# Two attention-and-mixer layers on one core: the planner's slack for VectorE units from 1000 to 0, and the last token tiles' normalization from VectorE to ScalarE

## The chip, the cores and the metric

The kernel runs on one core of a Trainium2 chip. The metric is the device time of one execution in microseconds. A run before the change took 1726.44 us (median of three executions, 1724.27 to 1726.56).

## What is computed

The reference applies the same pair of blocks twice, with the same weights, to one sequence of 2048 tokens with 640 features (`@` is a matrix product, all inputs are bf16):

```python
def A(x, wqkv, wo):                    # 32 heads of 20 features
    q, k, v = split(x @ wqkv)
    p = softmax(q @ k.T * 20 ** -0.5)  # per head, 2048 x 2048
    return concat_heads(p @ v) @ wo
def B(x, w1, b1, w2, b2):              # a token mixer: the products run over the 2048 tokens
    u = gelu(einsum("sd,sf->df", layernorm(x), w1) + b1)   # 1536 wide, tanh form
    return (u @ w2 + b2).T
x = x + A(layernorm(x)); x = x + B(layernorm(x))
x = x + A(layernorm(x)); x = x + B(layernorm(x))
```

## The kernel before

**The order of the work is planned in Python.** While the program is built, a planner keeps one clock per engine (`clk`), lists of jobs with a priority, a ready time and an assumed duration (`push`), and picks again and again the engine and the job that can start first; among jobs that can start at nearly the same time the lower priority number goes first (`queue_choose`, `pe_choose`). The instructions are emitted in that order, and on the chip each engine runs its own list in order, waiting on semaphores. So a constant of the planner costs nothing by itself, but it can change the order of everything that follows.

**Attention.** The scores of a layer are cut into 512 units. A unit is one query block of 512, one group of 4 heads and one tile of 128 keys, and it has 4 chunks of 128x512, one for each head of the group. Sixteen units with the same query block and group are a segment (the last segment of a layer is split into two halves by queries; the first segments of a layer are also cut, by keys). All P·V products of a segment (L927) add up in one PSUM bank, so P·V of the next segment starts only after VectorE has transposed that bank out (`f_tr`, L977). A unit's exponentials are made by one of two engines:

- *ScalarE* takes units in order; an instruction (`do_exp`, L887) does three or two chunks and writes them to one of 4 buffers `P`. Each chunk then needs one P·V matmul.
- *VectorE* takes whole units, chosen by `d_take`. It scales the 4 chunks out of PSUM (`do_J`, L840) into one of 3 buffers, and then makes 5 terms whose bit patterns, read as bf16, sum to the exponential (`do_T`, L860), each in one of 4 buffers `TT`. Each chunk needs five P·V matmuls. A term's buffer is free again after its four P·V matmuls.

**`d_take`** runs whenever fewer than two units are open and a score buffer is free. It adds up when VectorE would be done with another unit (`eta`), and gives it the first untaken unit of the earliest segment in which ScalarE would still be busy then:

```python
eta = (max(clk["DVE"], clk["PE"]) + (4 * 600.0 + NTERM * 610.0) * (d["open"] + 1) + len(t_jobs) * 610.0
       + sum(e[3] for e in jobs["DVE"]) + D_SLACK)
while si < NSEG and si <= acc["si"] + 1:
    if eta <= act_end(si): ...        # take untaken(si)[0]
    si += 1
```

`act_end(si)` is ScalarE's clock plus 453 ns for each chunk left up to the end of segment `si`, and `acc["si"]` is the segment whose P·V is under way. A unit that would be late for one segment is thus taken from the next.

**The end of a layer's attention.** When a segment is done, `normalize` transposes (`f_tr`), divides (`f_rec`, `f_mul`) and transposes back (`f_tr2`, L1012); `outproj` (L1066) multiplies by `wo` and adds the residual (L1105). Each token tile of 128 then gets its layer norm in `mix_ln`: statistics on VectorE (`stats_job`, L343 to L346), the scale `rt` and, where asked for, the shift `nmr` on GpSimd (`scale_job`, L354 to L360), and the normalized tile `h2`. Tiles 0 to 11 are long done by then; tiles 12 to 15 are the last four, 14 and 15 come after the last P·V. These two are normalized on VectorE straight from mean and scale (L1182), all others on GpSimd (L1190). Four matmuls for each pair of a hidden tile and a column half (`add_mm1_last`) then use the four tiles, VectorE adds the saved partial sums (L1325), ScalarE applies gelu (L1337), and the second product (`add_mm2`) runs on TensorE to the end of the layer. `gelu_table` (L1167 to L1170) makes ScalarE load its gelu table as soon as the last exponential is issued.

Of the kernel before, what the change touches and what calls it, by code (L numbers as in the profile page):

```python
# [14 lines left out]
ACT = mybir.ActivationFunctionType  # L15
ALU = mybir.AluOpType
# [51 lines left out]
LAT_ACT = 200.0  # L68
LAT_V = 120.0
EXP_CH = 453.0  # L70
D_SLACK = 1000.0
WIN_S = ((160.0, 160.0), (160.0, 160.0), (330.0, 160.0))
FILL_OVER = 0.0
M_F = 0.0
# [52 lines left out]
def kernel(  # L127
# [135 lines left out]
    def push(eng, prio, ready, dur, fn, ok=None, table=None):  # L263
        seq[0] += 1
        jobs[eng].append((prio, ready, seq[0], dur, fn, ok, table))
# [81 lines left out]
            then(mv, start + 950 + LAT_V)  # L347
        push("DVE", prio, ready, 950, f)

    def scale_job(prio, ready, mv, then, double, shift=True):  # L350

        def f(start):
            rt = stat.tile([128, 1], F32, name="rt")
            nc.gpsimd.tensor_scalar(out=rt[:], in0=mv[:, 1:2], scalar1=(1.0 + LN_EPS) if double else 1.0,  # L354
                                    scalar2=LN_EPS * LN_EPS if double else LN_EPS, op0=ALU.mult, op1=ALU.add)
            nc.gpsimd.tensor_tensor(out=rt[:], in0=rt[:], in1=mhalf[:], op=ALU.pow)
            nmr = None
            if double and shift:
                nmr = stat.tile([128, 1], F32, name="nmr")
                nc.gpsimd.tensor_scalar(out=nmr[:], in0=mv[:, 0:1], scalar1=rt[:, 0:1], scalar2=-1.0, op0=ALU.mult, op1=ALU.mult)  # L360
            then(rt, nmr, start + cost + 150)
        cost = 1100 if double and shift else 900
        push("POOL", prio, ready, cost, f)


    def add_fill(mms, cost, evac, ecost, ready=0.0, pr=5, ok=None, urgent=None, acost=None, eprio=2, bf16=None, on_start=None,
# [270 lines left out]
    def make_attention(L):  # L637
# [270 lines left out]
        def do_PV(start, sel):  # L908
            si = acc["si"]
            hist.append((start, 1.0))  # L910
            if acc["tile"] is None:
                acc["tile"] = ps(6, [128, 512])
            last = {}
            for it in sel:
                j = it[2]
                acc["cnt"][j] += 1
                last[j] = unassigned[si] == 0 and acc["cnt"][j] * 4 == pv_total[si]
            for part in range(2):
                for it in sel:
                    _, u, j, ap, ready, rel = it  # L920
                    qb, g, kt, half = units[u]
                    if half is None and part:
                        continue
                    dst, n = acc["tile"][32 * j:32 * j + 32, :], ((kt + part) * H + 4 * g + j) * VW
                    if half is not None:
                        dst, ap = dst[:, 0:256], ap[:, 256 * part:256 * (part + 1)]
                    pe(nc.tensor.matmul(dst, lhsT=Vaug[:, n:n + 32], rhs=ap, start=acc["cnt"][j] == 1 and not part,  # L927
                                        stop=last[j] and (half is None or part == 1), tile_position=(0, 32 * j)))
            for it in sel:
                pv.remove(it)  # L930
                pv_done[si] += 1
            end = start + PE_MM
            for it in sel:
                it[5](end)
            clk["PE"] = end
            pe_mode[0] = "col"
            if unassigned[si] == 0 and pv_done[si] == pv_total[si]:
                finish_seg(si, acc["tile"], end + LAT_PE)
                acc.update(si=si + 1, tile=None, cnt=[0] * 4, ready=1e18)
                if si + 1 == NSEG:  # L940
                    L.done = True
                    L.gelu_table()
                    if not L.nxt and L.w2_open:
                        for i in range(4, 8):
                            rW2.give(i, end + LAT_PE)
# [23 lines left out]
        def normalize(qb, g, half, src, ready, from_acc):  # L969
            final = half == 1  # L970
            q0, q1 = (0, 512) if half is None else (256 * half, 256 * half + 256)
            w = q1 - q0

            def f_tr(start):
                s1 = rT1.take()
                T1 = sb("T1", [128, w], F32, s1)
                nc.vector.transpose(out=T1[:], in_=src[:, 0:w])  # L977
                if from_acc:
                    acc["ready"] = start + 720 + LAT_V
                else:  # L980
                    sv_open[0] -= 1
                    if sv_open[0] == 0:
                        for i in range(NT_BUFS - NTSV, NT_BUFS):
                            rTT.give(i, start + 600)
                T1v = T1[:].rearrange("p (c i) -> p c i", i=32)

                def f_rec(start):
                    rden = stat.tile([128, 16], F32, name="rden")[:, 0:w // 32]
                    nc.vector.reciprocal(out=rden, in_=T1v[:, :, DH])  # L989

                    def f_mul(start):
                        s2 = rT2.take()
                        T2 = sb("T2", [128, w // 32, 32], BF16, s2)
                        eng = nc.vector if final else nc.gpsimd
                        end_ = start + (600 if final else 1450)
                        o_, a_, b_ = T2[:], T1v, rden.unsqueeze(2).to_broadcast([128, w // 32, 32])
                        if half is None:

                            o_ = o_.rearrange("p c i -> p (c i)").rearrange("p (c i b) -> p c b i", b=2, i=32)
                            a_ = T1[:].rearrange("p (c b i) -> p c b i", b=2, i=32)  # L1000
                            b_ = rden.rearrange("p (c b) -> p c b", b=2).unsqueeze(3).to_broadcast([128, w // 64, 2, 32])
                        eng.tensor_tensor(out=o_, in0=a_, in1=b_, op=ALU.mult)  # L1002
                        rT1.give(s1, end_)

                        def f_tr2(start):
                            if (qb, g) not in attnT:
                                aslot[(qb, g)] = rA.take()
                                attnT[(qb, g)] = sb("attnT", [128, 512], BF16, aslot[(qb, g)])
                            o_, i_ = attnT[(qb, g)][:, q0:q1], T2[:].rearrange("p c i -> p (c i)")
                            if half is None:  # L1010
                                o_, i_ = o_.bitcast(F32), i_.bitcast(F32)
                            nc.vector.transpose(out=o_, in_=i_)  # L1012
                            rT2.give(s2, start + 340)
                            on_normal(qb, g, half, start + 340 + LAT_V)
                        push("DVE", 0 if half is not None else 3, end_, 340, f_tr2, ok=lambda: len(rA) > 0 and L.v_left[1] == 0)
                    if final:
                        push("DVE", 0, start + 150, 600, f_mul, ok=lambda: len(rT2) > 0)
                    else:
                        push("POOL", 0, start + 150 + LAT_V, 1300, f_mul, ok=lambda: len(rT2) > 0)
                push("DVE", 1, start + 720, 170, f_rec)  # L1020
            push("DVE", 0, ready, 720, f_tr, ok=lambda: len(rT1) > 0)
# [109 lines left out]
    def make_mixer(L):  # L1131
# [28 lines left out]
        def got_last(tt, t):  # L1160
            h2l_ready[tt - NS_] = t
            L.mix_left -= 1
            if L.mix_left == NL - 1:
                add_mm1_last()
                add_mm2()

        def gelu_table():  # L1167
            nc.scalar.activation(out=warm[:, 0:1], in_=mhalf[:, 0:1], func=ACT.Gelu_apprx_tanh, scale=1.0)
            act_table[0] = "gelu"
            clk["ACT"] += 1500  # L1170

        def mix_ln(tt, x1s, ready, release):
            last = tt >= NS_

            def got_stats(mv, r):
                scale_job(1, r, mv, lambda rt, nmr, r2: apply_(mv, rt, nmr, r2), True, shift=not (last and L.done))

            def apply_(mv, rt, nmr, r):
                if nmr is None:
                    def f(start):  # L1180
                        h2[tt] = sb("h2", [128, D], BF16, tt)
                        nc.vector.tensor_scalar(out=h2[tt][:], in0=x1s[:], scalar1=mv[:, 0:1], scalar2=rt[:, 0:1],  # L1182
                                                op0=ALU.subtract, op1=ALU.mult)
                        got_last(tt, start + 550 + LAT_V)
                    push("DVE", 0, r, 550, f)
                    return

                def f(start):
# [5 lines left out]
                        release(e)  # L1194
                    (got_last if last else got_h2)(tt, e + 150)
                push("POOL", 1, r, 900, f, ok=(lambda: L.hT_dead) if tt >= NA1 else None)

            stats_job(3 if not last else 1 if L.done else 6, ready, x1s, got_stats)

        def add_mm1(k, tts):  # L1200

# [214 lines left out]
            if L.nxt:  # L1416
                L.nxt.load_wv()

        L.gelu_table = gelu_table
        L.on_hT_dead, L.mix_ln, L.on_attnT_dead, L.keys_dead = on_hT_dead, mix_ln, on_attnT_dead, keys_dead  # L1420


# [256 lines left out]
```

## Time and profile before

| | us |
|---|---|
| runs: median (lowest, highest) | 1726.44 (1724.27, 1726.56) |
| the profiled execution: its own time | 1724.27 |
| its span, first to last instruction | 1722.5 |
| TensorE busy, of the span | 1646.1 |
| ScalarE busy | 1581.0 |
| VectorE busy | 1464.6 |
| GpSimd busy | 167.5 |
| granted TensorE clock, mean | 0.995 |

PE is TensorE, PEld its weight loads, DVE VectorE, ACT ScalarE, POOL GpSimd. A row of the groups reads: line, engine, operation, output<-input tiles and their sizes, count | busy us, mean ns of one | idle time of the engine just before them, and what ended it. Instructions of an engine overlap a little, so busy time over count is a better spacing than the mean. A row of a timeline reads: start, duration, engine, line, operation, tiles, count, and in brackets the idle time before it.

In the span, attention of the first layer runs from about 24 to 798 us and of the second from about 850 to 1648 us; the mixer's last part follows each (798 to 850 us, and 1648 us to the end).

### The profile page before, as it was taken

The numbers are of one execution on the slowest core, as the hardware profiler recorded it, in microseconds if no ns is written. First come the engines' busy times: TensorE is split into PE (matmuls) and PEld (weight loads), VectorE is DVE, ScalarE is ACT, GpSimd is POOL, SyncE is SP. The second block draws the span as 40 slices with busy tenths as digits, with TensorE's granted clock in tenths as the row PEclk, the third lists the DMA queues.
The fourth block names the chain that finished last, engine by engine and source line by source line (L and its number), as shares of the span: only waits on it lengthen the run. The fifth ranks groups of instructions, "written<-read, shape, count | busy, mean of one in ns | idle before, by whom it ended". The sixth has DMA issues, their size and how long they took to land. (4 is left out here: it accounts for less than half of the span.)

```text
span 1722.5 us, 50500 instructions
## 1 busy us (share of the span) xinstructions
PE 1646.1 (96%) x21916; PEld 641.2 (37%) x21917; DVE 1464.6 (85%) x2630; ACT 1581.0 (92%) x1427; POOL 167.5 (10%) x261
## 2 busy tenths in 40 slices
PE   8999999999999999998999999999999999998989
PEld 3433333332333333335545432333333333332356
DVE  6688999999989999999444489999999888999963
ACT  7899999999999999997598899999999999999950
POOL 3100002000200020001100000110011000200010
PEclk9999999999999999999999999999999999999999
DMA  3200001000112106511422000100002120257143
GB/s 119 29 2 2 2 13 36 2 1 2 52 57 71 39 32 190 182 34 43 148 84 75 25 2 2 33 32 1 1 17 58 57 70 32 76 179 216 42 125 95
DMA packets 103295, 98.06 MB, mean 57 GB/s; under 512 B 45600, under 2 KB 79520, under 8 KB 103072
## 3 DMA queue, kind: packets, MB, share of 16 engines
q1 hardware_dynamic: 99456, 94.82, 17.8%
q8 instruction: 171, 2.80, 0.7%
q0 software_dynamic: 3616, 0.01, 0.3%
q14 instruction: 52, 0.43, 0.1%
HBM read 63.35 MB, written 31.46 MB: 55 GB/s over the span
## 5 line engine op out<-in xcount | busy, mean ns | idle before, releaser
L887 ACT ACTIVATE P<-pst 128x1536 bf16<-128x1536 f32 (+1 forms) x1335 | 1520.2, 1311 | 26.9 <-PE pst L700 14.5
L860 DVE TENSOR_SCALAR JT<-JT 128x2048 uint16<-128x2048 uint16 x950 | 636.4, 701 | 5.0 <-PE pst L927 1.8
L700 PE MATMUL pst<-QT,KT 32*128 32x512 bf16 (+1 forms) x4224 | 575.2, 377 | 40.7 <-ACT P L887 28.5
L840 DVE TENSOR_SCALAR JT<-pst 128x512 uint16<-128x512 f32 x760 | 507.4, 679 | 63.9 <-PE pst L700 61.5
L927 PE MATMUL pst<-P,Vaug 128*32 128x512 bf16 (+1 forms) x3440 | 500.6, 380 | 3.4 <-DVE T_85 L977 1.8
L927 PE MATMUL pst<-JT,Vaug 128*32 128x512 bf16 (+1 forms) x3920 | 465.7, 380 | 3.4 <-DVE T_85 L977 2.4
L700 PEld LDWEIGHTS <-KT 32*128 32x128 bf16 x4224 | 168.5, 91 | 512.2 <-issue 498.5
L927 PEld LDWEIGHTS <-Vaug 128*32 128x32 bf16 x7360 | 170.2, 94 | 297.3 <-issue 268.0
L1002 POOL TENSOR_TENSOR T_86<-T_85,rden 128x512 bf16<-128x512 f32 x64 | 67.5, 1054 | 1130.6 <-DVE rden L989 1090.8
L1066 PE MATMUL pst<-wo,attnT 128*32 128x320 bf16 x2048 | 111.3, 301 | 4.7 <-DVE attnT L1012 3.2
L456 PEld LDWEIGHTS <-W 128*32 128x32 bf16 x3384 | 89.7, 96 | 60.0 <-issue 28.8
L1488 PE MATMUL pst<-ident,zw 128*32 128x512 bf16 (+1 forms) x330 | 108.8, 380 | 0.0
L456 PE MATMUL pst<-hh,wq 128*32 128x512 bf16 x1232 | 104.3, 382 | 1.3 <-DVE JT L840 0.7
L456 PE MATMUL pst<-hh,wk 128*32 128x512 bf16 x1240 | 97.3, 381 | 1.1 <-DVE JT L840 0.6
L456 PE MATMUL pst<-x1last,W 128*32 128x320 bf16 x1536 | 80.6, 301 | 0.9 <-DVE JT L840 0.5
L1066 PEld LDWEIGHTS <-attnT 128*32 128x32 bf16 x2048 | 52.4, 96 | 42.2 <-issue 20.3
L456 PE MATMUL pst<-attnT,hh 128*32 128x320 bf16 x1196 | 60.2, 300 | 2.1 <-DVE hh L463 0.7
L463 DVE CAST KT<-pst 128x512 bf16<-128x512 f32 x53 | 36.0, 680 | 19.5 <-PE pst L456 18.3
L456 PE MATMUL pst<-JT,W 128*32 128x320 bf16 x1080 | 52.3, 300 | 0.0
L977 DVE STREAM_TRANSPOSE T_85<-pst 128x512 f32<-128x512 f32 (+1 forms) x58 | 40.0, 690 | 8.1 <-PE pst L927 8.0
L354 POOL TENSOR_SCALAR rt<-mv 128x1 f32<-128x1 f32 x64 | 13.4, 209 | 340.2 <-DVE mv L346 339.6
L463 DVE CAST Vaug<-pst 128x320 bf16<-128x320 f32 x43 | 20.6, 482 | 30.4 <-PE pst L456 21.6
(91 smaller groups left out, 878.0 us busy)
## 6 DMA issues: line engine op xcount, KB each, us to landing
W<-in_B_w_dram SPq DMA_DIRECT2D x10, 768.0 KB
W<-in_B_w_dram SPq DMA_DIRECT2D x24, 256.0 KB
xs<-in_A_x_dram SPq DMA_DIRECT2D x32, 160.0 KB
x2d<-xs SPq DMA_DIRECT2D x16, 320.0 KB
xs<-x2d SPq DMA_DIRECT2D x16, 320.0 KB
x1d_69<-xs SPq DMA_DIRECT2D x12, 320.0 KB
uacca_72<-W SPq DMA_DIRECT2D x12, 320.0 KB
W<-uacca_72 SPq DMA_DIRECT2D x12, 320.0 KB
```

The lines of the kernel that those rows point to most:

```text
L354: nc.gpsimd.tensor_scalar(out=rt[:], in0=mv[:, 1:2], scalar1=(1.0 + LN_EPS) if double else 1.0, scalar2=LN_EPS * LN_EPS if double else LN_ ...
L456: nc.tensor.matmul(out_[32 * c:32 * c + 32], lhsT=lhsT[:, 32 * c:32 * c + 32], rhs=rhs, start=start, stop=stop, tile_position=(0, 32 * c))
L463: nc.vector.tensor_copy(out=out_, in_=in_)
L700: pe(nc.tensor.matmul(dst, lhsT=k_, rhs=q_, start=True, stop=True, tile_position=(32 * j, 0)))
L840: nc.vector.tensor_scalar(out=c["jt"][:, j * 512:(j + 1) * 512], in0=Dt[:], scalar1=SCALE * LOG2E * 256.0, scalar2=127.0 * 256.0, op0=ALU. ...
L860: nc.vector.tensor_scalar(out=tt_[:], in0=c["jt"][:], scalar1=0.5, scalar2=TERM_C[i], op0=ALU.mult, op1=ALU.add)
L887: nc.scalar.activation(out=P[:, 0:n, :].rearrange("p a b -> p (a b)"), in_=St[:, 0:n, :].rearrange("p a b -> p (a b)"), func=ACT.Exp, scal ...
L927: pe(nc.tensor.matmul(dst, lhsT=Vaug[:, n:n + 32], rhs=ap, start=acc["cnt"][j] == 1 and not part, stop=last[j] and (half is None or part = ...
L977: nc.vector.transpose(out=T1[:], in_=src[:, 0:w])
L1002: eng.tensor_tensor(out=o_, in0=a_, in1=b_, op=ALU.mult)
L1066: nc.tensor.matmul(t[32 * c:32 * c + 32, 0:w], lhsT=q_, rhs=wo_pad[:, gg, c0:c1], start=(gi == 0), stop=(gi == len(gs) - 1), tile_position ...
L1488: pe(nc.tensor.matmul(dst[0:32, 0:128 * n], lhsT=zw[:, 0:32], rhs=ident[:].unsqueeze(1).to_broadcast([128, n, 128]), start=not inside, sto ...
```

## The change

1. `D_SLACK`, a term of `eta` in `d_take`, goes from 1000 to 0.
2. `h2` of the tiles that are normalized after the last P·V is made by ScalarE (an Identity activation with a scale and a bias for each partition) in place of VectorE; for that the shift `nmr` is needed for them too.
3. `nmr` is made by two GpSimd instructions (a product, then a multiplication by -1) in place of one.
4. The gelu table is asked for after the last of these four tiles has been normalized, in place of after the last P·V.
5. Priorities in VectorE's list: `f_tr2` of the two half segments goes from 0 to 3, and the statistics of last tiles that come before the last P·V from 6 to 1.

```diff
-D_SLACK = 1000.0
+D_SLACK = 0.0
...
 def scale_job
-                nc.gpsimd.tensor_scalar(out=nmr[:], in0=mv[:, 0:1], scalar1=rt[:, 0:1], scalar2=-1.0, op0=ALU.mult, op1=ALU.mult)
+                nc.gpsimd.tensor_tensor(out=nmr[:], in0=mv[:, 0:1], in1=rt[:], op=ALU.mult)
+                nc.gpsimd.tensor_scalar(out=nmr[:], in0=nmr[:], scalar1=-1.0, scalar2=None, op0=ALU.mult)
...
 def do_PV
                 if si + 1 == NSEG:
                     L.done = True
-                    L.gelu_table()
...
 def normalize
-                        push("DVE", 0 if half is not None else 3, end_, 340, f_tr2, ok=...)
+                        push("DVE", 3, end_, 340, f_tr2, ok=...)
...
 def got_last
                 add_mm1_last()
                 add_mm2()
+            if L.mix_left == 0:
+                nc.scalar.activation(out=warm[:, 0:1], in_=mhalf[:, 0:1], func=ACT.Gelu_apprx_tanh, scale=1.0)
+                act_table[0] = "gelu"
+                clk["ACT"] += 1500
...
 def mix_ln, apply_
-                if nmr is None:
+                if last and L.done:
-                        nc.vector.tensor_scalar(out=h2[tt][:], in0=x1s[:], scalar1=mv[:, 0:1], scalar2=rt[:, 0:1],
-                                                op0=ALU.subtract, op1=ALU.mult)
-                        got_last(tt, start + 550 + LAT_V)
-                    push("DVE", 0, r, 550, f)
+                        nc.scalar.activation(out=h2[tt][:], in_=x1s[:], func=ACT.Identity, bias=nmr[:, 0:1], scale=rt[:, 0:1])
+                        got_last(tt, start + 730 + LAT_ACT)
+                    push("ACT", 0, r, 730, f)
...
-            stats_job(3 if not last else 1 if L.done else 6, ready, x1s, got_stats)
+            stats_job(3 if not last else 1, ready, x1s, got_stats)
```

More of the change, by code (lines that the diff above doesn't have):

```diff
@@ L348, in stats_job, with scale_job @@
         push("DVE", prio, ready, 950, f)
-    def scale_job(prio, ready, mv, then, double, shift=True):
+    def scale_job(prio, ready, mv, then, double):
         def f(start):
@@ L357, in f @@
             nmr = None
-            if double and shift:
+            if double:
                 nmr = stat.tile([128, 1], F32, name="nmr")
-                nc.gpsimd.tensor_scalar(out=nmr[:], in0=mv[:, 0:1], scalar1=rt[:, 0:1], scalar2=-1.0, op0=ALU.mult, op1=ALU.mult)
-            then(rt, nmr, start + cost + 150)
-        cost = 1100 if double and shift else 900
-        push("POOL", prio, ready, cost, f)
+                nc.gpsimd.tensor_tensor(out=nmr[:], in0=mv[:, 0:1], in1=rt[:], op=ALU.mult)
+                nc.gpsimd.tensor_scalar(out=nmr[:], in0=nmr[:], scalar1=-1.0, scalar2=None, op0=ALU.mult)
+            then(rt, nmr, start + (1250 if double else 900) + 150)
+        push("POOL", prio, ready, 1250 if double else 900, f)
     def add_fill(mms, cost, evac, ecost, ready=0.0, pr=5, ok=None, urgent=None, acost=None, eprio=2, bf16=None, on_start=None,
@@ L1014, in f_tr2 @@
                             on_normal(qb, g, half, start + 340 + LAT_V)
-                        push("DVE", 0 if half is not None else 3, end_, 340, f_tr2, ok=lambda: len(rA) > 0 and L.v_left[1] == 0)
+                        push("DVE", 3, end_, 340, f_tr2, ok=lambda: len(rA) > 0 and L.v_left[1] == 0)
                     if final:
@@ L1165, in got_last @@
                 add_mm2()
[L1167 to L1170, printed above, removed]
+            if L.mix_left == 0:
+                nc.scalar.activation(out=warm[:, 0:1], in_=mhalf[:, 0:1], func=ACT.Gelu_apprx_tanh, scale=1.0)
+                act_table[0] = "gelu"
+                clk["ACT"] += 1500
         def mix_ln(tt, x1s, ready, release):
@@ L1175, in got_stats, with apply_ @@
             def got_stats(mv, r):
-                scale_job(1, r, mv, lambda rt, nmr, r2: apply_(mv, rt, nmr, r2), True, shift=not (last and L.done))
-            def apply_(mv, rt, nmr, r):
-                if nmr is None:
+                scale_job(1, r, mv, lambda rt, nmr, r2: apply_(rt, nmr, r2), True)
+            def apply_(rt, nmr, r):
+                if last and L.done:
                     def f(start):
                         h2[tt] = sb("h2", [128, D], BF16, tt)
-                        nc.vector.tensor_scalar(out=h2[tt][:], in0=x1s[:], scalar1=mv[:, 0:1], scalar2=rt[:, 0:1],
-                                                op0=ALU.subtract, op1=ALU.mult)
-                        got_last(tt, start + 550 + LAT_V)
-                    push("DVE", 0, r, 550, f)
+                        nc.scalar.activation(out=h2[tt][:], in_=x1s[:], func=ACT.Identity, bias=nmr[:, 0:1], scale=rt[:, 0:1])
+                        got_last(tt, start + 730 + LAT_ACT)
+                    push("ACT", 0, r, 730, f)
                     return
@@ L1417, in on_attnT_dead @@
                 L.nxt.load_wv()
-        L.gelu_table = gelu_table
         L.on_hT_dead, L.mix_ln, L.on_attnT_dead, L.keys_dead = on_hT_dead, mix_ln, on_attnT_dead, keys_dead
```

## The prediction

> **What bounds the kernel now.** I read the page's busy times first, then its groups, then a table of two long stretches of attention, then ScalarE's waits in one of them.
>
> ```profile
> PE 1646.1 (96%) x21916; PEld 641.2 (37%) x21917; DVE 1464.6 (85%) x2630; ACT 1581.0 (92%) x1427; POOL 167.5 (10%) x261
> ...
> L887 ACT ACTIVATE P<-pst 128x1536 bf16<-128x1536 f32 (+1 forms) x1335 | 1520.2, 1311 | 26.9 <-PE pst L700 14.5
> L860 DVE TENSOR_SCALAR JT<-JT 128x2048 uint16<-128x2048 uint16 x950 | 636.4, 701 | 5.0 <-PE pst L927 1.8
> ...
> L840 DVE TENSOR_SCALAR JT<-pst 128x512 uint16<-128x512 f32 x760 | 507.4, 679 | 63.9 <-PE pst L700 61.5
> ...
> L1488 PE MATMUL pst<-ident,zw 128*32 128x512 bf16 (+1 forms) x330 | 108.8, 380 | 0.0
> ```
>
> TensorE's 96% is no bound: 108.8 us of it are matmuls on zeros (L1488), issued where it had nothing to do. ScalarE's exponentials are 1520.2 us. There are 1024 units; 760 scaled chunks at 4 a unit make 190 units on VectorE, so ScalarE has 834 units, 3336 chunks, 1520.2 / 3336 = 0.456 us each and 1.82 us a unit. On VectorE a unit takes 4 x 507.4/760 + 5 x 636.4/950 = 2.67 + 3.35 = 6.02 us.
>
> ```profile
> 150.00:798.00 648.00, 623.62 (x8249) 216.53 (x8244) 615.18 (x1070) 639.12 (x564) 60.37 (x80) 0.99 0.16 49
> 1000.00:1648.00 648.00, 621.78 (x8232) 218.93 (x8230) 606.81 (x1057) 639.88 (x563) 59.20 (x82) 1.00 0.19 57
> ```
>
> The columns are the stretch, its length, then busy time (and instructions) of PE, PEld, DVE, ACT and POOL. In 1296 us ScalarE is idle for 8.9 + 8.1 = 17.0 us, VectorE for 32.8 + 41.2 = 74.0 us. ScalarE is the bound here, with VectorE close behind. The time can change in three ways: units move between the two, ScalarE waits more, or the stretches outside attention change.
>
> ```profile
> ACT P L887 <- PE pst L927: 4.2, 8, 1.2
> ACT P L887 <- PE pst L700: 4.0, 8, 1.2
> ```
>
> These are ScalarE's waits from 150 to 798 us: total, times, longest. It waits for P·V to free a P buffer (L927) or for scores queued behind P·V on TensorE (L700). The second layer has 6.8 us in 17 waits, so a wait is 15.0 / 33 = 0.45 us.
>
> **The slack.** Its unit is planned at 4 x 600 + 5 x 610 = 5.45 us and takes 6.02, so the chip falls 0.57 us behind the plan with each unit, 1.1 us with two open. The slack of 1.0 us covers that. Here is the end of a segment where it did not:
>
> ```profile
> 1264.83 8.23 ACT L887 ACTIVATE P<-pst 128x1536 bf16<-128x1536 f32 x7
> ...
> 1269.26 1.89 DVE L860 TENSOR_SCALAR JT<-JT 128x2048 uint16<-128x2048 uint16 x3
> ...
> 1271.22 0.61 PE L927 MATMUL pst<-JT,Vaug 128*32 128x512 bf16 x8
> ...
> 1272.26 0.71 DVE L977 STREAM_TRANSPOSE T_85<-pst 128x512 f32<-128x512 f32 x1
> ...
> 1273.02 0.40 PE L927 MATMUL pst<-P,Vaug 128*32 128x512 bf16 x4 [0.65 <-DVE T_85 L977]
> ...
> 1273.77 2.37 ACT L887 ACTIVATE P<-pst 128x1024 bf16<-128x1024 f32 x2 [0.72 <-PE pst L700]
> ```
>
> The segment's last exponential ends at 1269.5, its last VectorE term at 1271.15, the transpose starts at 1272.26, and the next segment's first P·V at 1273.02. ScalarE ran ahead on its 4 buffers and then stood still for 0.72 us. I went through the timeline in this way for the 54 whole segments between 143 and 776 us and between 992 and 1627 us (a segment's chunks are counted off its P·V matmuls). In 8 the last term ends 0.1 to 1.7 us after the last exponential. At 18 starts of a segment the opposite is seen: a unit put into the next segment has its fifth term held until 3.5 to 4.2 us after the last exponential of the segment before, since only 4 term buffers exist and none is freed before the next P·V opens.
>
> How many decisions change: a unit changes its segment where its planned end lies in the last 1.0 us before `act_end`. A segment takes about 23.4 us and holds 3.3 units, so units end 7.1 us apart: 1.0/7.1 x 54 = 8. All 18 held units are the upper bound; I take 10, between them and nearer to 8. Each now ends its segment at the planned end of ScalarE or just before it, which on the chip is later by the lag of 0.57 to 1.1 us. The segment's transpose, all P·V of the next segment behind it on TensorE, and the P buffers that these free come later by as much. ScalarE's 4 buffers hide some of it: the price is between 0 and 1.0 us each, and ScalarE's wait of 0.45 us is the nearest row; I take 0.4. That is 10 x 0.4 = +4.0 us, with 0 and 18 us as ends. The gain on the other side, units no longer held, is the third case below. The slack does not decide whether a unit is taken in the middle of a layer: a unit refused for one segment goes to the next, where 20 us and more are left. Only at a layer's end can a unit be won, at most one each.
>
> **The last tiles' normalization.** The end of the second layer, by engine:
>
> ```profile
> 1653.14 0.19 POOL L354 TENSOR_SCALAR rt<-mv 128x1 f32<-128x1 f32 x1 [3.75 <-DVE mv L346]
> 1653.42 0.55 POOL L356 TENSOR_TENSOR rt<-rt,mhalf 128x1 f32<-128x1 f32 x1
> ...
> 1654.36 0.56 DVE L1182 TENSOR_SCALAR hh<-x1last,mv,rt 128x640 bf16<-128x640 f32 x1
> 1655.63 0.61 DVE L1182 TENSOR_SCALAR hh<-x1last,mv,rt 128x640 bf16<-128x640 f32 x1 [0.72 <-POOL rt L356]
> ...
> 1654.97 11.68 PE L453 MATMUL pst<-hh,KT 128*128 128x320 bf16 x84 [1.75 <-DVE hh L1182]
> ...
> 1649.52 0.20 ACT L1168 ACTIVATE warm<-mhalf 128x1 f32<-128x1 f32 x1
> 1657.61 4.76 ACT L1337 ACTIVATE JT<-hh,b_t 128x640 bf16<-128x640 f32 x6 [7.89 <-issue]
> ```
>
> TensorE waits for tile 14 until 1654.97; then it has nine matmuls of 0.139 us that need only tile 14, which carries it to tile 15 at 1656.24. From there it never stops, so what delays tile 15 delays the end. New chain: GpSimd's power for tile 14 ends at 1653.97. The product (one-element GpSimd product in the set-up: 0.19 us) and the multiplication by -1 (0.19 as L354 to 0.26 as L360) with two gaps of 0.09 end at 1654.61. Tile 15's statistics are there at 1654.44; scale, power, product and multiplication take 0.19 + 0.55 + 0.20 + 0.26 with gaps of 0.09 and end at 1656.2. ScalarE takes the 0.83 us of the gelu rows, the same shape with a bias for each partition, and ends at 1657.03: 0.8 us later than 1656.24. The first layer's end has the same spacing (its two VectorE normalizations stand at 804.03 and 805.30), so 2 x 0.8 = +1.6 us. Below: 2 x 0.4 if the product hides in gaps. Above: a gelu chain that becomes late, next.
>
> **The gelu table** is loaded from 1648.22 for 1.28 us, and the first gelu is at 1657.61, so 8 us cover it. Now it starts behind tile 15: 1657.03 + 1.28 + 0.20 = 1658.5, when the first gelu, moved by 0.8, would be due at 1658.4. It costs 0.1 us, which the chain's later waits for VectorE (0.26 us before each of the last gelus) take up: nothing. The Trainium skill ("ScalarE: Activation LUTs", What ACT_TABLE_LOAD costs) puts a switch at 1.28 us of load and 1.38 us of drain; the row shows the load and the next activation 0.02 us behind it. By the page the tails would cost up to 1.4 us more each, 2.8 in all. The same page (Table sets) says that cheap functions such as identity stand in every set, so Identity would bring no load of its own; copies and casts run here between exponentials with no load, and Identity itself is in no row.
>
> **The other edits.** The second `nmr` instruction on the 28 tiles that have one today adds 0.3 us each to GpSimd, 10% busy, and none of these tiles is the one waited for; without that cover it would be 8 us. The half segments' `f_tr2` at priority 3 still goes ahead of scaling (4) and terms (5); at 1649.85 it has no rival. The earlier statistics of tiles 12 and 13 can push the last terms back by 0.95 us, but these end 3.0 and 6.5 us before the layers' last exponentials. All three: nothing.
>
> **Sum.** 1724.27 + 4.0 + 1.6 = 1729.9 us for the profiled execution. The median of the runs is 2.17 us above that execution, so the forecast is 1732.0 us.
>
> **Rivals.** *Covered:* the P buffers take up the late ends, or few decisions fall into the band, so that the constant does next to nothing; only the tail is left: 1726.4 + 1.6 = 1728.0. For it: of the 8 segments that end late today, several are followed by no wait of ScalarE. Against it: VectorE is idle for at most 0.1 us a segment from 310 to 444 us and from 1183 to 1250 us, so a late term is not caught up there. *More units:* the held fifth terms are the one mechanism on the other side. A unit finished in its own segment frees its score buffer 2 to 3 us earlier, the next is taken sooner, and VectorE, with 74 us idle, fills up. A further unit is worth 1.82 us, so one pays for the tail and three make 1726.4 + 1.6 - 5.5 = 1722.5, faster by over 0.2%. Against it: only 5.0 us of VectorE's idle time stands before terms, 61.5 us stand before scaling for scores that TensorE has not made. It decides from a count of 193 units, that is 772 scaled chunks.
>
> **How the numbers follow.** About 0.2% (3.5 us) is what a measurement of this kernel can tell from no change. Late ends 0.56, covered 0.28, more units 0.16. Of the first case a little lies within 0.2%, of the third a little too: slower 0.57, same 0.30, faster 0.13. The range goes from 1722.0 (three units won) to 1742.0 (14 late ends at the full 1.0 us, and the tail).
>
> **What would show it.** Right: about 190 units in L840 and L860, more ScalarE waits in the two stretches (21 us in place of 17), more segments with a term after the last exponential, Identity on ScalarE ending 0.8 us later after the statistics than today. Wrong: unit counts off by more than two, which would move the time by 1.82 us each whatever the waits do; a table load before Identity; or TensorE idle between the tiles and the first gelu by over 1 us more.

## The result and the profile after

The medians of four runs each are 1735.36 us (1733.46 to 1737.1) after, 1725.62 us (1724.27 to 1726.56) before. The ratio is 1.0057, with 1.0039 to 1.0074 as its 95% interval: 9.7 us slower. The profiled execution took 1737.1 us, its span is 1735.3 us. The forecast was 1732.0, and slower.

These are the rows of the page after the change that answer to those of before:

```profile
PE 1647.0 (95%) x21922; PEld 638.4 (37%) x21923; DVE 1462.6 (84%) x2625; ACT 1585.5 (91%) x1432; POOL 177.3 (10%) x297
...
L887 ACT ACTIVATE P<-pst 128x1536 bf16<-128x1536 f32 (+1 forms) x1335 | 1520.4, 1315 | 34.1 <-PE pst L700 22.9
L860 DVE TENSOR_SCALAR JT<-JT 128x2048 uint16<-128x2048 uint16 x950 | 636.5, 701 | 5.2 <-PE pst L927 1.6
```

Still 950 terms, so 190 units, and ScalarE's exponentials cost what they did. ScalarE's idle time ahead of them grew from 26.9 to 34.1 us. GpSimd has 36 instructions and 9.8 us more. The same two stretches of attention, columns as in the prediction:

```profile
150.00:798.00 648.00, 621.08 (x8207) 213.76 (x8196) 606.88 (x1057) 637.41 (x562) 60.12 (x88) 0.99 0.16 49
1000.00:1648.00 648.00, 616.89 (x8144) 213.52 (x8141) 605.48 (x1049) 637.22 (x560) 63.69 (x88) 0.99 0.19 56
```

ScalarE is idle for 10.6 + 10.8 = 21.4 us in them, against 17.0 before. That is the 21 us that the prediction named as its sign. But the kernel with the new slack alone (`e1_slack0`, below) shows this in the same stretches:

```profile
150.00:798.00 648.00, 620.16 (x8253) 215.52 (x8245) 608.15 (x1064) 641.41 (x566) 61.69 (x84) 1.00 0.16 49
1000.00:1648.00 648.00, 619.19 (x8259) 216.37 (x8256) 606.48 (x1060) 642.22 (x566) 62.24 (x80) 1.00 0.18 56
```

That is 6.6 + 5.8 = 12.4 us, less than before. So the sign came true, and not by the edit it was meant to show. The experiments had to find which edit it was.

One edit was not priced at all in the prediction: the shift's two instructions are also *planned* at 1250 ns in place of 1100 in `scale_job`, a line that the shortened diff leaves out. A planned duration costs nothing itself, but it can change the order of what follows.

### The profile page after: what moved, and what is told of

Its sections match the earlier page's. It is cut to its first block, busy times and chain, and to the rows that moved or that the text cites. A ratio compares the mean times of both kernels' runs of the same rounds, so it can differ in the third digit from the quotient of the medians.

```text
span 1735.3 us, 50531 instructions
## 1 busy us (share of the span) xinstructions
PE 1647.0 (95%) x21922; PEld 638.4 (37%) x21923; DVE 1462.6 (84%) x2625; ACT 1585.5 (91%) x1432; POOL 177.3 (10%) x297
## 3 DMA queue, kind: packets, MB, share of 16 engines
q1 hardware_dynamic: 99456, 94.82, 17.7%
## 4 chain that ended last, share of the span: by engine, by line
PE 47%; DVE 25%; ACT 18%; issue 8%; DMA 1%; POOL 0%; SPq 0%; DVEq 0%; POOLq 0%; ACTq 0%
ACT P L887 18%; PE pst L700 13%; PE pst L927 12%; PE pst L456 12%; DVE JT L860 10%; DVE JT L840 9%; PE pst L453 6%; PE pst L1065 2%; DVE T_85 L976 1%; DMA W<-in_B_w_dram 1%; PE pst L1483 1%; DVE QT L463 1%; DVE xs L1094 0%; DVE attnT L1011 0%; DVE W L1246 0%
## 5 line engine op out<-in xcount | busy, mean ns | idle before, releaser
L887 ACT ACTIVATE P<-pst 128x1536 bf16<-128x1536 f32 (+1 forms) x1335 | 1520.4, 1315 | 34.1 <-PE pst L700 22.9
L927 PE MATMUL pst<-P,Vaug 128*32 128x512 bf16 (+1 forms) x3440 | 508.6, 380 | 5.4 <-DVE T_85 L976 3.1
L927 PE MATMUL pst<-JT,Vaug 128*32 128x512 bf16 (+1 forms) x3920 | 481.0, 379 | 2.8 <-DVE T_85 L976 1.2
L456 PE MATMUL pst<-hh,W 128*32 128x320 bf16 x768 | 43.8, 308 | 8.1 <-DMA W<-in_B_w_dram 4.6
L354 POOL TENSOR_SCALAR rt<-mv 128x1 f32<-128x1 f32 x64 | 12.4, 193 | 336.5 <-DVE mv L346 335.8
L463 DVE CAST QT<-pst 128x512 bf16<-128x512 f32 x58 | 39.0, 673 | 8.3 <-PE pst L456 8.1
```

The source lines that it names most:

```text
L456: nc.tensor.matmul(out_[32 * c:32 * c + 32], lhsT=lhsT[:, 32 * c:32 * c + 32], rhs=rhs, start=start, stop=stop, tile_position=(0, 32 * c))
L463: nc.vector.tensor_copy(out=out_, in_=in_)
L887: nc.scalar.activation(out=P[:, 0:n, :].rearrange("p a b -> p (a b)"), in_=St[:, 0:n, :].rearrange("p a b -> p (a b)"), func=ACT.Exp, scal ...
```

## The experiments

Times are medians less the median of the kernel before on the same chip (1724.23, 1725.57 and 1724.76 us for the three groups), with the ratio of the runs and its 95% interval. That ratio is not the quotient of the two medians: read as microseconds it lies up to 1.2 us from the difference given.

### First group: one edit at a time

`e1_slack0` is the kernel before with only

```diff
-D_SLACK = 1000.0
+D_SLACK = 0.0
```

> The kernel before with D_SLACK 0 and nothing else. Late-ends theory (units planned up to the last exponential end a segment late on the chip, and ScalarE pays): the changed kernel without its tail cost of about 2 us, so 7 to 8 us over before, ratio 1.004, with about 15 segments whose last VectorE term ends after the last exponential (8 before), still 190 units, and two tails as long as before. Tail theory (the end of each layer is most of it): within 2 us of before. Reshuffle theory (any new order of the plan costs or gains a few us, without a direction): anything from -5 to +8 us, without a link to the number of late ends.

Measured: +1.4 us, 1.0007 [0.9998, 1.0016]. The late ends are there: of the 54 whole segments, 15 in place of 8 have their last term after the last exponential, and 6 in place of 18 units are held. The decisions changed about as often as forecast; their price did not appear.

`e5_tail_only` is the kernel before with tiles 14 and 15 as the change has them, and the gelu table behind them; the other tiles keep their one-instruction shift:

```diff
+            if two:
...
+                nc.gpsimd.tensor_tensor(out=nmr[:], in0=mv[:, 0:1], in1=rt[:], op=ALU.mult)
+                nc.gpsimd.tensor_scalar(out=nmr[:], in0=nmr[:], scalar1=-1.0, scalar2=None, op0=ALU.mult)
...
-                    L.gelu_table()
...
+                        nc.scalar.activation(out=h2[tt][:], in_=x1s[:], func=ACT.Identity, bias=nmr[:, 0:1], scale=rt[:, 0:1])
```

> The kernel before with tiles 14 and 15 normalized on ScalarE (shift by two GpSimd instructions) and the gelu table asked for behind them; slack and priorities as before, so that TensorE's and SyncE's orders stay the same. Prediction: 2 x 0.8 = +1.6 us, up to +2.2 us with the halved TensorE clock that the changed kernel shows once in each layer's end (about 0.3 us each); ratio 1.001. Tail theory: +6 us or more. If the halved clock comes from the longer pause of TensorE for tile 14, it shows here too, at the same two places; if it comes from the order before it, it does not.

Measured: +3.6 us, 1.0021 [1.0012, 1.003]. That is more than the 1.6 to 2.2 us expected and less than the 6 of the tail theory. In its profile the two layer ends are 2.4 and 1.2 us longer than before, and attention is as long as before. The halved clock is at both ends here too (from 805.2 and 1651.7 us), so it does not need the new order.

`e2_after_slack1000` is the change without its first edit:

```diff
-D_SLACK = 0.0
+D_SLACK = 1000.0
```

> The changed kernel with D_SLACK back at 1000: all of the change but the slack. Late-ends theory: +1.6 to +2.5 us over before, with 8 late ends. Reshuffle theory: its two-instruction shift and its priorities also alter the plan from late in the first layer on, so up to 5 us either way on top.

Measured: +2.2 us, 1.0012 [1.0004, 1.0021]. The slack alone is +1.4, all the rest alone is +2.2, and both together are +9.7. Six microseconds belong to neither: they come from the combination.

`e4_slack2000` is the kernel before with the slack moved the other way:

```diff
-D_SLACK = 1000.0
+D_SLACK = 2000.0
```

> The kernel before with D_SLACK 2000. Late-ends theory: no more than 4 late ends, more units held for the next segment, and ScalarE waits less in the middle of the layers: 0 to 3 us faster than before unless held units leave VectorE with fewer than 190 units (1.82 us each). Reshuffle theory: as far from before as slack 0 is, on either side, although late ends become fewer.

Measured: +2.6 us, 1.001 [1.0001, 1.0018]. Only one segment ends late here (8 before), and 20 units are held. But this run does not test late ends alone, for its page has 940 terms where the kernel before has 950:

```profile
L887 ACT ACTIVATE P<-pst 128x1536 bf16<-128x1536 f32 (+1 forms) x1338 | 1522.3, 1313 | 26.6 <-PE pst L700 14.0
L860 DVE TENSOR_SCALAR JT<-JT 128x2048 uint16<-128x2048 uint16 x940 | 632.1, 702 | 5.3 <-PE pst L927 2.0
```

VectorE has lost two units, 188 in place of 190: the case that the expectation excepted. ScalarE's exponentials take 2.1 us longer (1520.2 before), and at the prediction's 1.82 us a unit it would be 3.6 us. So the two units can account for most or all of the +2.6 us. Seven late ends fewer are then worth between a loss of 0.5 us and a gain of 1.0 us, an estimate; this run can't show more.

### Second group: the two-instruction shift, taken apart at slack 0

`f1_after_again` is the changed kernel, unedited, beside the next three.

> The changed kernel once more, beside the other three on one chip. It was 9.7 us over before, while slack alone made 1.4 and the last normalization alone 3.6 (ratios 1.0007 and 1.0021), all of it without the slack 2.1. If costs add, it is 5 us over before here (1.003); if the whole is more than its parts, 8 to 10 us (1.005).

Measured: +10.9 us, 1.007 [1.0057, 1.0083].

`f2_slack_and_tail` has slack 0, tiles 14 and 15 as in the change, and for all other tiles the old shift in one instruction, planned at 1100:

```diff
-D_SLACK = 1000.0
+D_SLACK = 0.0
...
+        cost = 1250 if two else 1100 if double and shift else 900
...
```

> Slack 0 and the last normalization on ScalarE, but every other tile's shift by one GpSimd instruction planned at 1100 ns, as before. The orders of TensorE and SyncE are those of slack 0 alone. Adding theory: 1.4 + 3.6 = +5 us (1.003). Order theory (the planned cost of the two-instruction shift moves the last 200 us of the second layer's attention into a worse order, with the partial sums' loads asked for elsewhere): +4 to +5 us here, against +8 to +10 in the whole change.

Measured: +1.7 us, 1.0011 [1.0003, 1.002].

`f3_two_instr_planned_1100` is the change with the two instructions planned as the one was:

```diff
-            then(rt, nmr, start + (1250 if double else 900) + 150)
-        push("POOL", prio, ready, 1250 if double else 900, f)
+            then(rt, nmr, start + (1100 if double else 900) + 150)
+        push("POOL", prio, ready, 1100 if double else 900, f)
```

> The whole change with its two-instruction shift, but planned at the old 1100 ns: GpSimd does the extra work and TensorE's order is that of slack and tail alone up to the last layer's end. Order theory: as slack and tail alone, +4 to +5 us. Instruction theory (the extra GpSimd instructions themselves delay someone): as the whole change, +8 to +10.

Measured: +5.3 us, 1.0035 [1.0023, 1.0047].

`f4_one_instr_planned_1250` is the change with one instruction where it has two, in the change's order:

```diff
-                nc.gpsimd.tensor_tensor(out=nmr[:], in0=mv[:, 0:1], in1=rt[:], op=ALU.mult)
-                nc.gpsimd.tensor_scalar(out=nmr[:], in0=nmr[:], scalar1=-1.0, scalar2=None, op0=ALU.mult)
+                nc.gpsimd.tensor_scalar(out=nmr[:], in0=mv[:, 0:1], scalar1=rt[:, 0:1], scalar2=-1.0, op0=ALU.mult, op1=ALU.mult)
```

> The whole change with one GpSimd instruction for the shift, but planned at 1250 ns: all other engines' orders are those of the whole change. Order theory: as the whole change, +8 to +10 us, less up to 0.6 us for the two ends. Instruction theory: +4 to +5.

Measured: +7.2 us, 1.0045 [1.0033, 1.0057]. The four make a square, all at slack 0 and with the new last normalization:

| us over before | planned 1100 | planned 1250 |
|---|---|---|
| one instruction | +1.7 (f2) | +7.2 (f4) |
| two instructions | +5.3 (f3) | +10.9 (f1) |

The second instruction costs 3.6 or 3.7 us, the planned 1250 costs 5.5 or 5.6, and 1.7 + 3.6 + 5.5 = 10.8: in this square the two add up. (On the tiles normalized after the last P·V `f2` has two instructions planned at 1250 and `f4` has one.) `f2` came out below what either theory expected; `f3` and `f4` together show that both effects are there, each smaller than its theory said. Halved clocks do not explain the planned 1250 between `f2` and `f4`: the mean granted clock of their runs is 0.9935 and 0.9936. It is 0.9928 in `f3` and 0.9902 in `f1`. Within one kernel, over all runs on record, a run whose mean clock is lower by 0.001 takes 0.6 us longer on average; by that estimate the clock is 0.4 us of the 3.6 between `f2` and `f3`, 1.5 of the 5.6 between `f3` and `f1`, and 2.0 of the 3.7 between `f4` and `f1`.

*The planned duration.* `f1` and `f2` share the first 38,556 of their some 43,800 matmuls and weight loads, and put the same number of units into every segment but the last two halves. From there, at about 1495 us, they differ; loads of partial sums are asked for elsewhere in SyncE's list too. ScalarE's waits show the difference between 1500 and 1662 us. First the change (all engines; engine, line and what is waited for: total, times, longest), then `f3`, which has `f2`'s order up to the last layer's end:

```profile
PEld L456 <- DMA W<-in_B_w_dram: 2.6, 2, 1.7
ACT P L887 <- PE pst L927: 2.6, 3, 1.4
...
ACT P L887 <- PE pst L700: 1.8, 3, 0.9
```

```profile
ACT P L887 <- PE pst L700: 0.7, 2, 0.6
```

The kernel before, from 1500 to 1650 us, lies between them:

```profile
ACT P L887 <- PE pst L927: 2.2, 2, 1.3
PEld L456 <- DMA W<-in_B_w_dram: 1.5, 2, 1.2
...
ACT P L887 <- PE pst L700: 0.6, 2, 0.4
```

With the longer planned duration ScalarE waits 4.4 us, without it 0.7 us: 3.7 of the 5.5 us. Before, it waits 2.8 us, and the weight tile is late there as well. So the order of slack 0 had removed these waits, and the planned 1250 brings them back with 1.6 us more. In the change TensorE stands before a weight tile of the mixer whose DMA is late (2.6 us, at 1554 to 1568 us), ScalarE then lacks scores, and at 1639 and 1650 us it waits for P·V of segments whose last term ends 2.5 and 2.0 us after the last exponential: the late end of the prediction, in two places. Why that DMA is late was not tried.

*The instruction.* `f3` and `f2` have the same order, and ScalarE falls back in steps of 0.18 to 0.47 us at ends of query blocks, about 2.0 us in all. Here is such a place, GpSimd and VectorE of `f2`, then of `f3`:

```profile
445.79 0.26 POOL L364 TENSOR_SCALAR nmr<-mv,rt 128x1 f32<-128x1 f32 x1
446.00 1.05 POOL L1005 TENSOR_TENSOR T<-T,rden 128x512 bf16<-128x512 f32 x1
...
446.57 1.03 DVE L864 TENSOR_SCALAR JT<-JT 128x2048 uint16<-128x2048 uint16 x1
```

```profile
445.68 0.19 POOL L360 TENSOR_TENSOR nmr<-mv,rt 128x1 f32<-128x1 f32 x1
445.96 0.22 POOL L361 TENSOR_SCALAR nmr<-nmr 128x1 f32<-128x1 f32 x1
446.14 1.05 POOL L1001 TENSOR_TENSOR T<-T,rden 128x512 bf16<-128x512 f32 x1
...
446.48 1.26 DVE L860 TENSOR_SCALAR JT<-JT 128x2048 uint16<-128x2048 uint16 x1
```

The second instruction starts GpSimd's product `T` later, by 0.23 us relative to VectorE's term. The term, 0.68 us elsewhere, takes 1.03 us in one kernel and 1.26 us in the other; in both it ends 0.55 us after the product ends (447.60 - 447.05, 447.74 - 447.19). VectorE's term stands still until GpSimd's instruction is over. So a GpSimd that is busy for 10% does hold VectorE, which is what "nothing" overlooked. What that costs the kernel is not shown. Counted over the kernel, terms held in this way lose 14.5 us in `f2` and 16.3 in `f3`, 16.1 in `f4` and 17.6 in `f1`: +1.8 and +1.5 us beside the 3.6. But the kernel before loses 17.7 us in them, as much as `f1`, and is 10.9 us faster. The rest of the 3.6 is not seen in these rows; in this pair of profiles it lies at 689 us, where a weight tile is late in both and the clock is halved for longer in `f3`, and in the first layer's end (2.1 us), and stays open.

### Third group: dose, removal, and the layers' ends

`g1_four_instr_planned_1100` is `f3` with the shift in four GpSimd instructions:

```diff
                 nc.gpsimd.tensor_tensor(out=nmr[:], in0=mv[:, 0:1], in1=rt[:], op=ALU.mult)
-                nc.gpsimd.tensor_scalar(out=nmr[:], in0=nmr[:], scalar1=-1.0, scalar2=None, op0=ALU.mult)
+                for _ in range(3):
+                    nc.gpsimd.tensor_scalar(out=nmr[:], in0=nmr[:], scalar1=-1.0, scalar2=None, op0=ALU.mult)
```

> As the whole change with its shift planned at 1100 ns, but the shift in four GpSimd instructions (a product and three multiplications by -1); all other engines' orders are the same. Port theory (a VectorE term instruction waits while GpSimd works, so each instruction of GpSimd that is longer by 0.3 us makes VectorE, TensorE and ScalarE late by as much where they overlap): one instruction was 1.7 us over before, two 5.3, so four are 9 to 12 over (1.005 to 1.007), in steps of about 0.55 us at the ends of the query blocks. Chance theory (the 3.6 us were halved clocks that fell badly): 4 to 7 us, as with two.

Measured: +8.7 us, 1.0046 [1.0032, 1.0059]. One, two and four instructions in the same order give +1.7, +5.3 and +8.7 (the last in another group): the cost rises with the dose, to just under the 9 to 12 us of the port theory. But the time for which terms are held does not (14.6 us against `f2`'s 14.5). Nor does the profile show the 7.0 us between `f2` and `g1`: ScalarE's last exponential ends only 2.8 us later (1652.1 against 1649.3), and the profiled execution, 1731.2 us, is the fastest of `g1`'s. The extra instructions cost time at slack 0; that they do it by holding terms, as the port theory has it, is not shown, and the mechanism stays open.

`g2_no_shift_instr` is the kernel before, in its own order, with no shift instruction; the long GpSimd instruction takes mean and scale directly:

```diff
-                nmr = stat.tile([128, 1], F32, name="nmr")
-                nc.gpsimd.tensor_scalar(out=nmr[:], in0=mv[:, 0:1], scalar1=rt[:, 0:1], scalar2=-1.0, op0=ALU.mult, op1=ALU.mult)
+                nmr = mv
...
-                    nc.gpsimd.tensor_scalar(out=h2[tt][:], in0=x1s[:], scalar1=rt[:, 0:1], scalar2=nmr[:, 0:1],
-                                            op0=ALU.mult, op1=ALU.add)
+                    nc.gpsimd.tensor_scalar(out=h2[tt][:], in0=x1s[:], scalar1=mv[:, 0:1], scalar2=rt[:, 0:1],
+                                            op0=ALU.subtract, op1=ALU.mult)
```

> The kernel before without any shift instruction: GpSimd normalizes its tiles as (x - mean) x scale in its one long instruction; planned costs and all other engines' orders as before. Port theory: 1 to 3.6 us faster than before (0.998 to 0.9995). Chance theory: no difference.

Measured: +4.7 us, 1.0023 [1.0014, 1.0032]: a miss. The groups by form, before and then here:

```profile
L1190 POOL TENSOR_SCALAR x1last<-xs,rt,nmr 128x640 bf16<-128x640 f32 x16 | 16.9, 1059 | 1.5
```

```profile
L1189 POOL TENSOR_SCALAR x1last<-xs,mv,rt 128x640 bf16<-128x640 f32 x16 | 45.9, 2866 | 1.6
```

Subtract and multiply on the same tile takes 2.9 us where multiply and add takes 1.1, so this kernel has more GpSimd time (205.9 against 167.5 us), not less. As an accidental dose it points the same way: order unchanged, GpSimd busy for longer, and 4.7 us lost. Here too the held terms lose hardly more than before (18.3 against 17.7 us).

`g4_after_busy_ends` and `g5_no_shift_busy_ends` are the change and `g2` with TensorE's gaps at the layers' ends filled with more matmuls on zeros, since 14 of the 16 profiled ends that have the changed normalization show a halved clock just where the last tiles are waited for (5 of 8 without it):

```diff
-        if o[0] > now + 250 and sum(h[1] for h in hist) < HAM_MIN and now > 2000:
+        state.gap = o[0] - now
+        if o[0] > now + 250 and sum(h[1] for h in hist) < (16.0 if a is not None and a.done else HAM_MIN) and now > 2000:
...
+        reps = max(1, int(state.gap / 230.0)) if a.done else 1
+        for _ in range(reps):
+            pe(nc.tensor.matmul(dst[0:32, 0:128 * n], lhsT=zw[:, 0:32], rhs=ident[:].unsqueeze(1).to_broadcast([128, n, 128]), ...
...
```

> The changed kernel with eight more matmuls on zeros in each layer's end, where TensorE waits for the last segment's transposes; nothing else moves. If the halved clock that most profiles show about there comes from that pause and costs time, it is gone from both ends and the kernel is 1 to 3 us faster than the changed kernel, 8 to 10 over before; if it is set by something else, it stays, and the time is that of the changed kernel or up to 0.3 us more for matmuls that outlast the pause.

> The kernel before without shift instructions and with the eight matmuls on zeros in each end: the best that these runs point to. Port and clock together: 2 to 5 us faster than before (0.997 to 0.999); chance theory: no difference.

Measured: `g4` +11.7 us, 1.0067 [1.0052, 1.0082], no better than the change; `g5` +2.6 us, 1.0009 [1.0, 1.0018], a miss as well, 2.1 below `g2`, with overlapping intervals. In `g4`'s profile the halved clock is gone from that place at both ends (one window is left, at 840 us), the mean granted clock of its runs is 0.994 as in the kernel before (0.990 in `f1`), and the time is still the change's; so halved clocks at these pauses are not what the change pays. None of these kernels beats the one before.

## Why the prediction was right, and where it was not

**Direction and size came out, 1735.4 for 1732.0, but not by the step that carried them.** That the forecast came near was luck: the term that carried it is much smaller than forecast, and a term put at nothing made up for it. Term by term:

- *Units.* 190 before and after. Right, and "more units" fell.
- *The slack, +4.0.* This is the mis-sized term. Alone it measures +1.4 [-0.3, +2.8]. The count was about right (7 more late ends, 12 fewer held units, for 10 changed decisions). The price of 0.4 us each was not: by the median it is 1.4 / 7 = 0.2 for each late end that came, with an interval that includes nothing, and ScalarE's idle time in the two stretches fell by 4.6 us. The mean of ScalarE's waits was taken for the price of a late end, where it should have been the mean over all late ends, those without a wait included. The text had this as its rival, and `f2`, slack and last normalization together, is +1.7 (0.5 to 3.4 by its interval) where the covered rival's sum is +1.6. One reading of the rows was loose: the held fifth terms end 3.5 to 4.2 us after the last exponential; they start, and so are released, 2.3 to 3.3 us after it.
- *The last normalization, +0.8 at each layer's end.* The chain is as worked out:

```profile
1666.29 0.21 DVE L346 BATCH_NORM_AGGREGATE mv<-bnst 128x2 f32<-128x12 f32 x1
...
1667.91 0.23 POOL L361 TENSOR_SCALAR nmr<-nmr 128x1 f32<-128x1 f32 x1
...
1668.17 0.92 ACT L1180 ACTIVATE hh<-x1last,nmr,rt 128x640 bf16<-128x640 f32 x1 [0.60 <-POOL nmr L361]
1669.11 1.28 ACT L1166 ACT_TABLE_LOAD   x1
1670.40 0.20 ACT L1166 ACTIVATE warm<-mhalf 128x1 f32<-128x1 f32 x1
1670.51 4.69 ACT L1333 ACTIVATE JT<-hh,b_t 128x640 bf16<-128x640 f32 x6
```

  Tile 15's normalization ends 1669.09 - 1666.50 = 2.6 us after its statistics, against 1.8 before: +0.8. In time the two ends together are +0.2 beside slack 0 (`f2` less `e1`, across groups) and +3.6 alone (`e5`); 1.6 lies between, and the runs do not narrow it.
- *The gelu table, nothing.* Right. No load stands before Identity, one load of 1.28 us stands behind it, the next activation follows 0.01 us later and the first gelu 0.11 us after that one begins. The Trainium skill ("ScalarE: Activation LUTs", What ACT_TABLE_LOAD costs) adds 1.38 us of drain to each switch; no such gap shows here, so the row was the better guide.
- *"The other edits: nothing."* This step failed. The priorities are indeed nothing: with the old ones the change gives the same instructions in the same order. The shift is not. At slack 0 its second instruction costs 3.6 us and its planned duration 5.5 us, 9 of the 10.9. The argument was that GpSimd is 10% busy and none of these tiles is waited for. Both are true, and neither is enough: `scale_job`'s planned duration is an input to the order of everything behind it, and GpSimd's instructions can hold VectorE's, though by which way the second instruction costs its 3.6 us is open. The prediction named 8 us as the price without its cover, and no case contained it.
- *Adding the terms.* With slack 1000 all edits but the slack cost +2.2, with slack 0 they cost +8 to +9.5. `e2`, at slack 1000, has the planned 1250 and the second instruction on all tiles, and at +2.2 is no slower than `e5`, which has them on the last tiles alone, at +3.6. So in these runs both do harm only beside slack 0. A price for each edit of such a planner holds only beside the other edits.

Where the time is depends on the comparison, and a table of stretches needs that warning. From the profiles, in us; an attention ends with its last transpose out of PSUM, a layer's end with the next layer's first P·V, and second-layer attention is cut where its quarter-length segments end (about 992 us before) and eight segments before its end:

| | first layer's attention, end | second layer's attention: early, middle, late | its end |
|---|---|---|---|
| before | 798.8, 50.7 | 142.9, 491.2, 165.5 | 73.4 |
| e1, slack alone | 797.9, 50.0 | 144.2, 494.9, 161.1 | 75.1 |
| f2 | 799.0, 50.8 | 145.3, 494.9, 161.1 | 74.5 |
| f1, the change | 800.5, 51.1 | 144.5, 495.7, 165.2 | 75.4 |

Against before, the change loses in the early and middle part (+1.6, +4.5), and the late one is even. Against `f2`, its late part loses 4.1. Both are so: slack 0 places a unit into one of the cut segments at 975 us, where ScalarE then stands for 2.6 us in three waits, and changes which segments hold a fourth unit, with ends up to 3.4 us later; by the last segments its order has won that back, and the planned 1250 takes this gain away.

## What to carry to other kernels

A constant that only tells a planner how long something takes is an edit of the whole program: diff the order that comes out, and price the edits together, not one by one. An engine's low busy share says that it is not the bound, not that it disturbs nobody; look for the instructions of its neighbours that get longer beside its own. And a sign named in advance proves its mechanism only if the edit alone shows it: here 21 us of waits came as forecast, and the edit they were forecast for had lowered them.

## What the hardware showed that was not expected

**A lock, to within 20 ns.** In the kernel before, 59 of the 950 terms end 0.543 to 0.563 us after the end of a GpSimd instruction that they overlap, whatever their own duration (0.68 to 1.53 us; 45 are longer than 0.7). Together they take 17.7 us more than 59 undisturbed ones of 0.684 us; 15.3 of that stands behind the product `T`, 64 instructions of 1.05 us. The scaling, which reads PSUM, is not lengthened. The Trainium skill ("SBUF — State Buffer", Who interferes with whom) says that GpSimd and some VectorE modes share one port pair, held for a whole instruction, and that the second to come waits until the first is done. These rows agree: the held term ends only after the GpSimd instruction has ended. The change has 17.6 us of such loss, no more than the kernel before, so it is a price that both pay. Moving the product off GpSimd was not tried.

**Operations on GpSimd differ.** On 128x640, subtract and multiply took 2.87 us (mean; the shortest 2.51), multiply and add 1.06 (the shortest 0.87).

**The clock halves in steps.** Windows of 3.4 us, at times two in a row, on a grid of 3.41 us, have half the granted clock, and one program meets them at different places from run to run. They follow pauses of TensorE. Of the windows of this grid in the 14 profiles (100 to 1690 us, not halved themselves), 33 have TensorE busy for less than half, and 26 of these are followed by a halved one; between half and 0.8 it is 30 of 264, above 0.8 it is 1 of 6157. The change has one at 1662.2 us (the third column from the end is the granted clock, 1.00 in the same place before):

```profile
1662.00:1664.00 2.00, 1.90 (x28) 0.97 (x28) 1.42 (x5) 0.00 (x0) 0.00 (x0) 0.56 1.15 348
```

Runs of one kernel spread over 2 to 7 us, so the differences of 1 to 2 us here rest on the medians and not on single profiles.
